# Pooled attention with a three-way maximum layer: tile 5's output by half products, and tile 6's first layer beside batch 7's scores alone

## The chip, the cores and the metric

The kernel runs on one core of a Trainium2 chip. The metric is device time in microseconds (us) of one execution, as the median of several runs. Its engines work in parallel, each through its own queue in order, and wait for one another through semaphores: TensorE (PE in the profile, its weight loads PEld) multiplies matrices into PSUM banks, VectorE (DVE) and ScalarE (ACT) read those banks and write SBUF, GpSimd (POOL) works on SBUF alone, and SyncE (SP) and POOL issue DMAs.

## The reference

```python
# q, k, v: 8 batches x 8 heads x 576 tokens x 64
k_p = k.reshape(B, H, 72, 8, D).mean(axis=3)          # groups of eight keys pooled
v_p = v.reshape(B, H, 72, 8, D).mean(axis=3)
attn = softmax(q @ k_p.T / 8)
x = (attn @ v_p), heads side by side                  # 4608 tokens x 512
h = max(max(x @ w1, x @ w2), x @ w3)                  # 768 wide
out = h @ w_out                                       # 4608 x 512, float32
```

## The kernel before

**Two grids.** Attention goes by batch (0 to 7, 576 tokens each), the two layers behind it by tile (0 to 8, 512 tokens each). The layers of tile n run beside the attention of batch n + 1, so that TensorE always has something to do while ScalarE takes exponentials. For one batch there are a key turn (`k`: POOL's pooled keys are turned by TensorE, and VectorE and ScalarE copy them to `kz`), eight scores steps (`s0` to `s7`; in the last stage nine, `s70` to `s78`, of 512 columns) each with an exp on ScalarE, and five values steps (`v0` to `v4`): eight small matmuls into `pav`, then a reciprocal and a multiplication on VectorE give `xn`, and step `x` turns it into `xT` by a DMA transpose on SyncE's queue. POOL folds the keys and values (`k7+1`, `v6+2` and the like: so many of the three steps of a fold).

**The first layer.** x @ w1 is folded into the output: w2 and w3 have w1 subtracted, so that the maximum is taken against zero, and w1 @ w_out (`wm`) is added in the output layer. For tiles 0 to 5 the first layer goes by "hidden" steps (`h` in a stage's list, `hidden_part`): twelve for a tile, each four matmuls of 512 columns, into banks `pw`, with a relu on ScalarE or a maximum on VectorE.

**Seven products.** A product of two-by-two blocks can be had from seven block products and some sums (Winograd's form). Tiles 6, 7 and 8 have their first layer that way (`seven`, products 1 to 7 for each of three column groups a, b, c: in the order, `6b` is product 6 of group b). Each is four matmuls of 256 columns for each of two weights. Products 1, 6, 5 and 3 of a group add up in one bank (`pA`), which ScalarE copies out after each of them (L811, L815) before the next is added. Product 2 has a bank of its own, `pB`, which VectorE adds (L782). Products 7, 5 and 4 use `pC`: 7 fills it, after 5 and 7 VectorE adds it to 5's copy, then 4 is added to it and VectorE adds it to 6's copy. VectorE's maxima (L785) then write `hT`. The sums that the products read come from `fold_x`: on VectorE for tile 6 (`T`, `U`), on POOL for tiles 7 and 8 (`T`).

**The output layer.** Tile n's output is [x, h] @ [wm, w_out]. The old form, `project(n)`, goes by four chunks of 128 tokens, each four and six matmuls of 512 columns into a bank `po`, one ScalarE copy and two stores; a step of it is written `F` and is one of these two halves. The other form, `out_seven(n)`, has seven products of ten matmuls of 256 columns into banks `oA`, `oB`, `oC`, with ScalarE's copies of `oA` (L737) and VectorE's additions (L740); it needs eight sums of x and h on VectorE (`a1` to `a4`, `b1` to `b4`). Before, tiles 2, 3, 4, 7 and 8 have it, and tiles 0, 1, 5 and 6 have the old one.

**The order.** It is written out by hand. `MIDDLE[n]` lists the steps of tiles 1 to 4 and `middle(n)` runs them; in it a number is an output product, `2l` and `2h` the halves of product 2, `e2` and `e5` VectorE's late additions, `7:T` and `6:k` a step of another batch. Tile 5 has `block(5, LEAD, ...)`: its twelve hidden steps with batch 6's scores and first two values between them. Then the last stage ("the weave") runs `ORDER`: tile 6's products, batch 6's other values, batch 7's scores and values, tile 7's products and tile 8's, with old-style output steps `F` of tile 5 (eight) and of tile 6 (six, the rest at the end) between them.

**Banks.** PSUM has eight banks. In the weave `pA` has two, `pB` and the scores share two ("sc"), and `pC` and `po` have one each; values and tile 7's `oA` share the other two. The weave's banks lie over those of the stages before it (scores and values 4, `pw` with `oB` and `oC` 3, `oA` 1), so a first use there waits until the old tile has been read.

Of the kernel before, what the change touches and what calls it, by code (L numbers as in the profile page):

```python
# [14 lines left out]
def kernel(  # L15
# [15 lines left out]
    B, H, S, D = q.shape  # L31
# [30 lines left out]
    def psum(shape, dtype, name, tag, bufs):  # L62
        return pools[-1].tile(shape, dtype, name=name, tag=tag, bufs=bufs)
# [86 lines left out]
    def tokens(t0, t1, k0=0, k1=KCH):  # L150

        t0, t1 = t0 % RING, (t1 - 1) % RING + 1
        assert t0 < t1
        return xT[:, k0:k1, t0:t1]
# [248 lines left out]
    def new_two():  # L403
        return sb3.tile([128, 2, C], F32, name="osb", tag="osb", bufs=3)

    def project(n):
        hT = hTs[n]
        for mm in range(4):
            m = 4 * n + mm
            last = m == TOK // 128 - 9  # L410
            if mm % 2 == 0:
                two = new_two()
            osb = two[:, mm % 2]
            for c in ((slice(0, C // 2), slice(C // 2, C)) if last else (slice(0, C),)):
                tag = PW if len(pools) < 3 else PA if last else PO
                po = psum([128, c.stop - c.start], F32, name="po", tag=tag[0], bufs=tag[1])
                for kc in range(KCH):
                    nc.tensor.matmul(po, tokens(128 * m, 128 * m + 128)[:, kc], wm_sb[:, kc, c],  # L418
                                     start=(kc == 0), stop=False)
                yield  # L420
                for jc in (0, 3, 1, 4, 2, 5):
                    nc.tensor.matmul(po, hT[:, jc, bass.ts(mm, 128)], wo_sb[:, jc, c],  # L422
                                     start=False, stop=(jc == JCH - 1))
                if c.start:
                    nc.vector.tensor_copy(out=osb[:, c], in_=po)
                else:
                    nc.scalar.copy(out=osb[:, c], in_=po)  # L427
                for u in range(2):
                    b, g = divmod(2 * m + u, NG)
                    dst = out[S * b:S * b + S, :].rearrange("(r g) c -> r g c", g=NG)  # L430
                    (nc.scalar if last and u else nc.sync).dma_start(
                        out=dst[:, GS[g], c], in_=osb[64 * u:64 * u + 64, c])
            yield
# [89 lines left out]
    def block(n, plan, parts):  # L523

        for slot, _ in enumerate(part for stage in parts for part in stage(n)):
            for b, steps in plan.get(slot, ()):
                if b < B:
                    do(b, steps)
# [5 lines left out]
    PRODUCTS = FIRST | {3: ("S4", 3), 4: (3, "T4"), 5: ("S1", "T1"), 6: ("S2", "T2")}  # L534
    sw = {}

    LEAD = {0: [(6, "s0")], 1: [(6, "s1")], 2: [(6, "s2")], 3: [(6, "s3")],
            4: [(6, "s4")], 5: [(6, "s5")], 6: [(6, "s6")], 7: [(6, "s7")],
            8: [(6, "v0 x0")], 9: [(6, "v1 x1")]}

    def minus(out, a, b):
        gate[:] = [nc.vector.tensor_tensor(out=out, in0=a, in1=b, op=ALU.subtract)]

# [39 lines left out]
    LAST = TOK // NB - 1  # L583
# [254 lines left out]
    def pool_step(n, name):  # L838
# [19 lines left out]
            held.clear()  # L858

    ORDER = """  # L860
        1a k7 F F T 2a U 1b v62 s70 F s71 s72 6a F s73 v63 5a 7a s74 s75 v64 F s76
        4a s77 3a s78 6b 2b 7b 1c v70 2c 5b T F 6c v71 3b F 5c 4b F v72 7c 3c 1a
        F 1b 4c v73 2a 2b 6b 6a F v74 5a 7a F 3a F T 1c 4a 5b 2c 6c 7b 3b F 5c
        4b F 1a 7c 2a 3c 6a 4c H 1b 2b 5a 6b 7a 3a h o1 1c 4a o2 5b 6c 7b 2c o6
        4b 3b 5c o5 7c o7 4c 3c o3 o4
    """

    def weave():

        products, seen = {}, {}  # L870
        for name in ORDER.split():
            if name == "F":
                next(tiles)
            elif name == "H":
                fold_h(LAST - 1)
                outs = out_seven(LAST - 1)
            elif name == "h":
                fold_h(LAST - 1, True)
            elif name[0] == "o":
                outs(int(name[1]), 0, 1)  # L880
            elif name[0] in "ksvx":
                b = int(name[1])
                do(b, name[0] + name[2:])
                if name[0] == "v" and b > 2:
                    do(b, "x" + name[2:])
                if name[0] == "s" and name[2] == "4" and b + 1 < B:
                    do(b + 1, "T")
            else:
                n = seen[name] = seen.get(name, 5) + 1
                if n not in products:  # L890
                    products[n] = seven(n)
                products[n](*((0, name == "U") if name in "TU" else
                              (int(name[0]), "abc".index(name[1]))))
                if name == "U":
                    held[:] = gate
                    pool_step(n, "v7+2")
# [17 lines left out]
        4: """  # L914
            h k k7< q7< v7< h a1 a3 a2 a4 f ! v5+2 h h s0 h s1 h s2 h s3 h s4 b1 f ! k6+1 h s5
            h s6 h s7 h b2 b3 b4 f ! k6+2 v6+1
            1 v0 x0 2l v1 x1 7:T 6 7 v2 x2 5 v3 x3 e5 2h 6:k 3 v4 x4 e2 4 v6+2 k7+3 v7+1
        """}
    folds = iter([f for wi in range(1, 3) for f in [fold_w(wi)] * 4])

    def middle(n):

        pieces, outs, out_tiles = hidden(n), None, project(n)
        for name in MIDDLE[n].split():
            if name == "h":
                next(pieces)
            elif name == "F":
                next(out_tiles)
            elif name == "f":
                next(next(folds))  # L930
            elif name == "!":
                held[:] = gate
            elif name.isdigit():
                outs = outs or out_seven(n)
                outs(int(name), 0, 1)
            elif name in ("2l", "2h"):
                outs = outs or out_seven(n)
                outs(2, "lh".index(name[1]))
            elif name in ("e2", "e5"):
                outs(int(name[1]))  # L940
            elif name[0] in "ab":
                sums_of(n, name)
            elif name[2:3] in ("<", "+"):
                pool_step(n, name)
            else:
                b, _, step = name.rpartition(":")
                do(int(b or n + 1), step)
        assert next(pieces, None) is None

    tt_all.append(const.tile([128, 4, 5, HALF], F16, name="tt", tag="tt"))  # L950
    for n in range(1, 5):
        middle(n)
    block(5, LEAD, (hidden,))
    assert next(folds, None) is None
    pad2 = const.tile([128, 3, 2, HALF], F16, name="pad2", tag="k16")
    pad3 = ld.tile([128, 8, 2, HALF], F16, name="pad3", tag="vt")
# [3 lines left out]
    stage.close()  # L960
    pools.append(ctx.enter_context(tc.tile_pool(name="psq", bufs=1, space=PSUM,
                                                reuse_waits="tile")))
    tiles = (t for n in range(5, LAST - 1) for t in project(n))
    weave()
    outs = out_seven(LAST)
    fold_h(LAST)
# [35 lines left out]
```

## Time and profile before

| | |
|---|---|
| median of 3 runs | 224.29 us (224.13 to 224.95) |
| the profiled execution | 224.51 us, its span 222.8 us |
| granted TensorE clock, mean | 0.998 |
| busy share: PE, DVE, ACT, POOL | 96%, 67%, 55%, 63% |
| tile 4's hidden layer, its output | 119.95 to 132.54, 132.54 to 141.65 us |
| tile 5's hidden layer | 141.65 to 154.66 us |
| the weave | from 154.66 us |

The span is what the profiler saw from the first to the last instruction; the rest of an execution's time lies around it. Times in the rows are us from the span's start. A row of the timeline is start, length, engine, line, operation, output <- inputs, and in square brackets how long the engine had been idle and for whom. A row of the chain is start, length, engine, tile, line and count. In the rows "x4" counts instructions.

### The profile page before, as it was taken

How to read it: one execution, taken by the hardware profiler on the slowest of the kernel's cores; microseconds unless marked ns; L12 is line 12 of the kernel's file. 1: busy time of each engine (PE TensorE's matmuls, PEld its weight loads, DVE VectorE, ACT ScalarE, POOL GpSimd, SP SyncE). 2: the span in 40 equal slices, each digit the busy share in tenths (PEclk: the TensorE clock that was granted, in tenths of full speed). 3: DMA queues.
4: the chain of work that ended last, by engine and by line, in shares of the span. 5: the costliest groups of instructions: out<-in, count | busy, mean ns of one | idle time of the engine just before them, and what ended most of it. 6: DMA issues, size and time to landing. Idle time of an engine off the chain costs nothing.

```text
span 222.8 us, 4685 instructions
## 1 busy us (share of the span) xinstructions
PE 215.0 (96%) x1807; PEld 146.9 (66%) x1807; DVE 149.0 (67%) x292; ACT 122.3 (55%) x221; POOL 141.0 (63%) x115
## 2 busy tenths in 40 slices
PE   7898999999999999999999999999999999999993
PEld 2477744558755555875597569655687777788882
DVE  4658967037584385787488658827677887898840
ACT  2267534756875478337823863584786545564340
POOL 7975404999949767787858766999421904772020
PEclk9999999999999999999999999999999999999999
DMA  6999999999469999649999999865341623200265
GB/s 175 212 197 197 203 208 203 201 239 230 86 112 204 222 188 216 114 93 160 233 227 170 154 269 144 157 133 118 76 100 27 139 62 74 47 3 0 68 197 163
DMA packets 50726, 33.54 MB, mean 151 GB/s; under 512 B 27056, under 2 KB 46384, under 8 KB 50704
## 3 DMA queue, kind: packets, MB, share of 16 engines
q0 software_dynamic: 20320, 16.98, 48.6%
q1 hardware_dynamic: 29936, 15.87, 31.0%
q10 hardware_dynamic: 448, 0.39, 0.7%
q8 instruction: 14, 0.23, 0.4%
q14 instruction: 8, 0.07, 0.1%
HBM read 34.60 MB, written 9.44 MB: 198 GB/s over the span
## 4 chain that ended last, share of the span: by engine, by line
PE 90%; DVE 4%; DMA 3%; ACT 1%; issue 1%; SPq 0%
PE pw L368 27%; PE oA L727 10%; PE po L422 9%; PE pA L805 7%; PE po L418 6%; PE psc L220 6%; PE oC L727 5%; PE pav L270 4%; PE pC L805 4%; DMA ktTrue<-in_k_dram 3%; PE oB L727 2%; PE pm L355 2%; PE pB L805 2%; PE pxt L261 2%; PE pqt L194 1%; DVE xn L278 1%
## 5 line engine op out<-in xcount | busy, mean ns | idle before, releaser
L368 PE MATMUL pw<-xT,mw 128*128 128x512 f16 (+1 forms) x336 | 72.8, 348 | 0.4 <-ACT xT L264 0.2
L368 PEld LDWEIGHTS <-mw 128*128 128x128 f16 x336 | 31.6, 98 | 20.7 <-issue 0.9
L376 DVE TENSOR_TENSOR hT<-t,pw 128x512 f16<-128x512 f16 (+1 forms) x42 | 25.4, 609 | 23.0 <-ACT et L225 16.4
L225 ACT ACTIVATE et<-psc 72x576 f16<-72x576 f32 (+2 forms) x54 | 35.2, 660 | 6.6 <-PE psc L220 6.3
L164 POOL TENSOR_TENSOR half<-half 96x768 f32<-96x768 f32 (+2 forms) x14 | 27.4, 1956 | 13.7 <-DVE rcp L276 9.0
L163 POOL TENSOR_TENSOR half<-vt 72x2048 f32<-72x2048 f16 (+1 forms) x8 | 28.6, 3577 | 3.3 <-DMA vt<-in_v_dram 2.7
L374 ACT ACTIVATE t<-pw 128x512 f16<-128x512 f32 (+1 forms) x42 | 22.6, 537 | 14.8 <-PE pw L368 14.1
L278 DVE TENSOR_TENSOR xn<-pav,rcp 128x512 f16<-128x512 f32 x40 | 27.7, 692 | 1.4
L422 PE MATMUL po<-mwo,hT 128*128 128x512 f16 (+1 forms) x102 | 23.5, 366 | 0.0
L220 PE MATMUL psc<-qT,kz 128*128 128x320 bf16 (+2 forms) x120 | 22.4, 278 | 0.8 <-DVE qT L196 0.6
L220 PEld LDWEIGHTS <-kz 128*128 128x128 bf16 x143 | 13.1, 98 | 13.3 <-ACT qT L196 1.1
L163 POOL TENSOR_TENSOR half<-ktFalse 96x1536 f32<-96x1536 f16 x6 | 18.8, 3128 | 4.0 <-issue 2.9
L811 ACT CAST pad<-pA 128x512 f16<-128x512 f32 x27 | 15.5, 587 | 8.2 <-PE pA L805 8.1
L276 DVE RECIPROCAL rcp<-pav 128x8 f32<-128x8 f32 x40 | 8.2, 204 | 17.0 <-PE pav L270 16.7
L270 PEld LDWEIGHTS <-et 72*128 72x128 f16 x320 | 15.3, 98 | 3.5 <-issue 0.3
L571 POOL TENSOR_TENSOR pad<-xT 128x256 f16<-128x256 f16 x8 | 6.1, 757 | 17.2 <-PE pB L805 8.6
L270 PE MATMUL pav<-vp,et 72*128 72x65 f16 x320 | 16.6, 194 | 0.1
L418 PE MATMUL po<-wm,xT 128*128 128x512 f16 (+1 forms) x68 | 16.6, 366 | 0.0
L737 ACT COPY osb<-oA 128x512 f32<-128x512 f32 x12 | 7.0, 585 | 16.7 <-PE oA L727 16.7
L427 ACT COPY osb<-po 128x512 f32<-128x512 f32 (+1 forms) x16 | 9.2, 572 | 12.0 <-PE po L422 12.0
L785 DVE SCALAR_TENSOR_TENSOR hT<-pad 128x512 f16<-128x512 f16 x18 | 14.1, 798 | 2.3 <-ACT pad L815 1.9
L805 PEld LDWEIGHTS <-sw 128*128 128x128 f16 x144 | 13.7, 98 | 2.4
(122 smaller groups left out, 382.9 us busy)
## 6 DMA issues: line engine op xcount, KB each, us to landing
out_dram<-osb SPq DMA_DIRECT2D x38, 128.0 KB, 5.5
ktFalse<-in_k_dram POOLq DMA_DIRECT2D x7, 576.0 KB, 8.7
qb<-in_q_dram POOLq DMA_DIRECT2D x7, 576.0 KB, 12.7
vt<-in_v_dram POOLq DMA_DIRECT2D x6, 576.0 KB, 14.9
mw<-in_moe_w_dram POOLq DMA_DIRECT2D x9, 256.0 KB, 9.2
out_dram<-osb SPq DMA_DIRECT2D x8, 256.0 KB, 5.6
ktTrue<-in_k_dram SPq DMA_DIRECT2D x3, 384.0 KB, 5.0
vt<-in_v_dram POOLq DMA_DIRECT2D x4, 288.0 KB, 12.4
```

The lines of the kernel that those rows point to most:

```text
L163: yield e.tensor_tensor(out=f, in0=t[:, :, 0:4, :], in1=t[:, :, 4:8, :], op=ALU.add)
L164: yield e.tensor_tensor(out=f[:, :, 0:2, :], in0=f[:, :, 0:2, :], in1=f[:, :, 2:4, :], op=ALU.add)
L220: nc.tensor.matmul(out, kz_all[b % 2][f % 2][rows, h, :], qTs[b][rows, n + i0:n + i1, 64 * (h % 2):64 * (h % 2) + 64], start=True, stop=True)
L225: nc.scalar.activation(out=out, in_=in_, func=FT.Exp, scale=1.0 / 64.0)
L270: nc.tensor.matmul(pav[:, h // 4, 65 * (h % 4):65 * (h % 4) + 65], ets[b][:, h, c0:c0 + 128], vp_all[:, b, h, :], start=True, stop=True)
L278: nc.vector.tensor_tensor(out=xn, in0=pv[:, :, :, 0:D], in1=rcp.to_broadcast([128, 2, 4, D]), op=ALU.mult)
L368: mm = nc.tensor.matmul(pw, w_sb[wi][:, kc, bass.ts(jc, 128)], x[:, kc], start=(kc == 0), stop=(kc == KCH - 1))
L376: nc.vector.tensor_tensor(out=hT[:, jc, c0:c1], in0=t, in1=pw, op=ALU.max)
L418: nc.tensor.matmul(po, tokens(128 * m, 128 * m + 128)[:, kc], wm_sb[:, kc, c], start=(kc == 0), stop=False)
L422: nc.tensor.matmul(po, hT[:, jc, bass.ts(mm, 128)], wo_sb[:, jc, c], start=False, stop=(jc == JCH - 1))
L727: nc.tensor.matmul(p, left, right, stop=(r == 4), skip_group_check=True, start=(i in FIRST and r == 0 and (m == 0 or n == LAST)))
L805: mm = nc.tensor.matmul(p[:, w], a[:, kc, bass.ts(g, 128)], b[:, kc, :], start=(i in FIRST and w + kc == 0), stop=(w + kc == 2), skip_grou ...
```

## The change

Tile 5 loses its `LEAD` block and gets a list in `MIDDLE`, like tile 4's: hidden steps with batch 6's scores, the eight sums, then the seven output products with all five values of batch 6 and the key turn of batch 7 between them. The folds of values 6, keys 7 and values 7, which stood at the end of tile 4's list, stand in tile 5's. In the weave's `ORDER` the key turn, three values steps of batch 6 and the eight `F` steps of tile 5 are gone. Up to tile 6's product 4c no `F` is left: tile 6's products stand with batch 7's scores, later its first four values, and tile 7's first products. Tile 6's six `F` steps stand further on, with the gaps between them changed.

```diff
-    LEAD = {0: [(6, "s0")], 1: [(6, "s1")], 2: [(6, "s2")], 3: [(6, "s3")],
-            4: [(6, "s4")], 5: [(6, "s5")], 6: [(6, "s6")], 7: [(6, "s7")],
-            8: [(6, "v0 x0")], 9: [(6, "v1 x1")]}
-
...
     ORDER = """
-        1a k7 F F T 2a U 1b v62 s70 F s71 s72 6a F s73 v63 5a 7a s74 s75 v64 F s76
-        4a s77 3a s78 6b 2b 7b 1c v70 2c 5b T F 6c v71 3b F 5c 4b F v72 7c 3c 1a
-        F 1b 4c v73 2a 2b 6b 6a F v74 5a 7a F 3a F T 1c 4a 5b 2c 6c 7b 3b F 5c
-        4b F 1a 7c 2a 3c 6a 4c H 1b 2b 5a 6b 7a 3a h o1 1c 4a o2 5b 6c 7b 2c o6
+        1a T 2a U 1b s70 s71 6a s72 s73 5a 7a s74 s75 s76
+        4a s77 3a s78 6b 2b 7b 1c v70 2c 5b T 6c v71 3b 5c
+        4b v72 7c 3c 1a 1b 4c v73 2a 2b 6b F 6a v74 5a 7a F 3a F T 1c 4a 5b 2c 6c 7b 3b F 5c
+        4b F 1a 7c 2a 3c 6a F 4c H 1b 2b 5a 6b 7a 3a h o1 1c 4a o2 5b 6c 7b 2c o6
         4b 3b 5c o5 7c o7 4c 3c o3 o4
     """
...
         4: """
             h k k7< q7< v7< h a1 a3 a2 a4 f ! v5+2 h h s0 h s1 h s2 h s3 h s4 b1 f ! k6+1 h s5
             h s6 h s7 h b2 b3 b4 f ! k6+2 v6+1
-            1 v0 x0 2l v1 x1 7:T 6 7 v2 x2 5 v3 x3 e5 2h 6:k 3 v4 x4 e2 4 v6+2 k7+3 v7+1
+            1 v0 x0 2l v1 x1 7:T 6 7 v2 x2 5 v3 x3 e5 2h 6:k 3 v4 x4 e2 4
+        """,
+        5: """
+            h h a1 a3 a2 a4 ! v6+2 h h s0 h s1 h s2 h s3 h s4 b1 ! k7+1 h s5
+            h s6 h s7 h b2 b3 b4 ! k7+2 v7+1
+            1 v0 x0 2l v1 x1 6 7 v2 x2 5 v3 x3 e5 v4 x4 2h 7:k 3 e2 4
         """}
...
-    for n in range(1, 5):
+    for n in range(1, 6):
         middle(n)
-    block(5, LEAD, (hidden,))
...
-    tiles = (t for n in range(5, LAST - 1) for t in project(n))
+    tiles = project(LAST - 2)
     weave()
```

## The prediction

> **What bounds the kernel now.** I read the busy time by stretches first, for tile 4's hidden layer and output stage and the start of the weave, then the chain.
>
> ```profile
> 119.95:132.54 12.59, 12.59 (x71) 6.51 (x69) 8.00 (x16) 9.19 (x16) 9.20 (x7) 1.00 1.05 182
> 132.54:141.65 9.11, 9.09 (x114) 8.06 (x112) 8.16 (x18) 2.13 (x5) 6.53 (x4) 1.00 0.84 141
> ...
> 154.66:164.90 10.24, 10.24 (x96) 6.92 (x94) 6.99 (x15) 7.37 (x14) 5.48 (x3) 1.00 0.37 78
> 164.90:175.30 10.40, 10.40 (x100) 7.88 (x98) 8.33 (x15) 6.62 (x12) 3.51 (x5) 1.00 0.33 70
> ```
>
> The columns are length, then busy us of PE, PEld, DVE, ACT, POOL, then clock. TensorE fills every stretch, the weave from 154.66 too, where tile 6's products stand between the halves of tile 5's old-style output (po). So TensorE time saved is time saved, and a TensorE wait made is time lost. VectorE (6.99 of 10.24, 8.33 of 10.40) and ScalarE (7.37 at first) have room there only because po gives TensorE other work. The chain gives the unit prices:
>
> ```profile
> 132.54 1.09 PE oA L727 x10
> ...
> 157.82 0.44 PE pA L805 x4
> 158.26 0.26 PE pav L270 x8
> 158.52 0.22 PE psf L220 x2
> 158.74 0.86 PE po L418 x4
> ...
> 189.71 1.30 PE po L422 x6
> ```
>
> **TensorE's work.** Removed: tile 5's four po chunks, 4 x (0.86 + 1.30) = 8.64 us. Added: seven products of ten matmuls, 7 x 1.09 = 7.63. The three value steps (0.26 each) and the scores only move; the key turn is made earlier. Net -1.01 us.
>
> **Work that hides.** Tile 5's stage becomes a copy of tile 4's: hidden steps with scores, then products with values. It adds to VectorE eight sums and three additions, to ScalarE nothing (four copies for four). In tile 4's stretches the same work left VectorE at 8.00 of 12.59 and 8.16 of 9.11 with TensorE full, so I cost it at nothing; uncovered, it would cost up to that 8.16 us. POOL's folds of batches 6 and 7 move from ahead of that stage into it, as batches 5 and 6 lie in tile 4's: 9.20 of 12.59, nothing; their last two steps must land before batch 7's first values, 10 us into the weave, and the stretch from 154.66 shows them with slack. SyncE gets five transposes earlier and six stores for eight: nothing.
>
> **The entry of the weave.** Tile 4's output stage passes into a hidden layer with other banks. Tile 5's now passes into product 1a, whose bank (pA) is the one that tile 5's outputs (oA) leave: the built program makes 1a wait for ScalarE's last oA copy. Before, tile 4's end:
>
> ```profile
> 138.08 0.43 PE L270 MATMUL pav<-vp,et 72*128 72x65 f16 x8
> 138.79 0.69 DVE L278 TENSOR_TENSOR xn<-pav,rcp 128x512 f16<-128x512 f32 x1
> 139.40 0.68 DVE L740 TENSOR_TENSOR osb<-osb,oC 128x512 f32<-128x512 f32 x1
> 139.99 0.97 DVE L210 COPY kz<-pkt 64x288 bf16<-64x288 bf16 x2
> 140.99 0.21 DVE L276 RECIPROCAL rcp<-pav 128x8 f32<-128x8 f32 x1
> 141.24 0.69 DVE L278 TENSOR_TENSOR xn<-pav,rcp 128x512 f16<-128x512 f32 x1
> ...
> 141.33 0.97 ACT L210 COPY kz<-pkt 64x288 bf16<-64x288 bf16 x2 [2.46 <-DVE rcp L276]
> 142.32 0.58 ACT L737 COPY osb<-oA 128x512 f32<-128x512 f32 x1
> ```
>
> ScalarE's kz copies wait for VectorE's, and the oA copy is behind them: it ends at 142.90, 1.25 us after TensorE went on to tile 5's hidden layer at 141.65, where I set the end of that stretch. Nobody waited for it. Now 1a does: 1.3 us as the row stands. In the new order VectorE normalises the fifth values (0.21 + 0.69) before kz, at most 0.9 later, so 2.2 at most. Counted through, VectorE ends kz as product 4 ends; ScalarE follows at about 0.1 with 0.99, then 0.58, so 1a starts at 1.70. I take 1.7. Besides, the key turn now stands after the fifth values and takes the bank of the fourth's, so it waits for their xn: by the rows that ends 1.40 after the fourth values start (138.08 to 139.48), and TensorE comes there after 2 x 0.26 and half a product, 0.55, 1.07: 0 to 0.4 late, I take 0.4. **Entry: +2.1.**
>
> **Tile 6's products without po between.** What each step waits for is in the code and the built program. Products 1, 6, 5, 3 of a group sum up in one pA bank, each after ScalarE's copy of the one before. A group's 4 waits for VectorE's addition of 5+7, the next group's 7 for its addition of 4 (one bank). Two "sc" banks serve the scores and product 2, so a score waits for the exp (or addition) two users back. The latencies and rates:
>
> ```profile
> 21.32 0.58 ACT L264 COPY xT<-pxt 128x512 f16<-128x512 f16 x1 [0.22 <-PE pxt L261]
> 21.95 1.47 PE L368 MATMUL pw<-xT,mw 128*128 128x256 f16 x12 [0.19 <-ACT xT L264]
> ...
> 154.50 0.60 PE L805 MATMUL pA<-xT,mw 128*128 128x256 f16 x4
> 155.13 0.58 ACT L811 CAST pad<-pA 128x512 f16<-128x512 f32 x1 [0.70 <-PE pA L805]
> 157.22 0.60 PE L805 MATMUL pB<-xT,mw 128*128 128x256 f16 x4
> 157.93 0.69 DVE L782 TENSOR_TENSOR pad<-pad,pB 128x512 f16<-128x512 f16 x1 [0.67 <-PE pB L805]
> 158.34 0.58 ACT L811 CAST pad<-pA 128x512 f16<-128x512 f32 x1 [0.33 <-PE pA L805]
> 158.54 0.42 DVE L571 TENSOR_TENSOR pad<-xT 128x512 f16<-128x512 f16 x1
> 158.82 0.59 ACT L225 ACTIVATE et<-psf 72x512 f16<-72x512 f32 x1
> ```
>
> ScalarE starts 0.63 after a product starts (154.50 to 155.13), works 0.58, and TensorE goes on 0.05 after its end (21.90 to 21.95): 1.26 us from one product on a pA bank to the next, of which TensorE works 0.44. Queued behind each other, ScalarE starts an operation each 0.48 (158.34 to 158.82), VectorE each 0.61 (157.93 to 158.54).
>
> I count from the end of tile 5's product 4. 1a starts at 1.70, 2a at 2.14, 1b at 2.58, score 0 at 3.02. Score 1 needs 2a's bank: 1a's copy ends at 2.92, the addition at 3.66, so it starts at 3.71, **0.47 late**. 6a 3.93, score 2 4.37; score 3 needs score 1's exp, which stands behind 1b's copy and score 0's exp on ScalarE, until 4.84 (**0.25**); 5a needs 6a's copy, behind those, 5.32 (**0.26**). 7a, scores 4 and 5 are ready; score 6 needs score 4's exp, behind 5a's copy and two exps: 7.29 (**0.65**). 4a, 7, 3a, 8, 6b, 2b, 7b, 1c follow at 0.44 or 0.22 each, and the first values of batch 7 start at 10.6. Their predecessors are 12 x 0.44 + 9 x 0.22 = 7.26 us of work, so 3.35 are lost, 1.70 of them the entry. **+1.6.**
>
> From there VectorE sets the pace: each group wants three additions, two maxima and a normalisation. 3b waits 0.13, 5c 0.05, values 2 0.22 (bank of values 1), 7c **0.96** (the maximum of 3b, the normalisation and the addition of 4b are queued ahead), tile 7's 1b 0.39 (3c's copy), 6b 0.22 (POOL's sums of tile 7, below), 5a 0.57 (6a's copy, no po ahead of it). **+2.5.** Then po of tile 6 stands between products as before, and I add nothing. The sums of tile 7 go by
>
> ```profile
> 168.51 0.69 DVE L278 TENSOR_TENSOR xn<-pav,rcp 128x512 f16<-128x512 f32 x1
> 171.71 0.67 POOL L571 TENSOR_TENSOR pad<-xT 128x256 f16<-128x256 f16 x1 [8.59 <-ACT pad L811]
> 175.86 0.67 POOL L571 TENSOR_TENSOR pad<-xT,pad 128x256 f16<-128x256 f16 x1
> ```
>
> 2.5 us from batch 7's first xn (ends 169.20) through its transpose to the first sum, 4.8 to the end of the sixth (176.53), which 6b needs. The walk has that xn end at 12.0 after product 4, so the sixth sum ends at 19.3, 0.2 after TensorE comes to 6b.
>
> **Sum.** -1.0 + 2.1 + 1.6 + 2.5 = +5.2. The profiled execution took 224.51 (span 222.8 and 1.7 around it) against a median of 224.29: the span becomes 228.0, that execution 229.7, the median **229.5**.
>
> **Bounds of the unshown waits.** No stretch of before runs these products without po, so the engines' loads bound their cost from below. For a maximum there are two prices, beside POOL's sums and alone:
>
> ```profile
> 174.04 1.22 DVE L785 SCALAR_TENSOR_TENSOR hT<-pad 128x512 f16<-128x512 f16 x1
> 174.04 0.67 POOL L571 TENSOR_TENSOR pad<-xT,pad 128x256 f16<-128x256 f16 x1
> 178.64 0.69 DVE L785 SCALAR_TENSOR_TENSOR hT<-pad 128x512 f16<-128x512 f16 x1
> ```
>
> If VectorE never waited: two leftover additions 1.3, four sums at 0.42 1.7, nine additions at 0.68 6.1, six maxima at 0.69 4.1, three normalisations at 0.90 2.7 = 15.9 us, against TensorE's 13.1 to tile 7's 1b (23 products, 9 scores, 4 values); with the 0.61 spacing about 14.6. ScalarE: the leftover 1.65, 14 copies at 0.58, 9 exps at 0.59 = 15.1. So the least loss is 1.5 to 2.8, net of the 1.01 saved +0.5 to +1.8. The walk stands above since each wait starves the next engine. Upward goes the first price of a maximum (rival b).
>
> **Rivals.**
> (a) *Pure load*: queues run full ahead of TensorE and only the busier engine's total counts: the middle of the bounds, +1.2, 225.5. For it: additions and maxima of different groups are independent. Against: one pC bank and two sc banks forbid running ahead. Chance 0.12.
> (b) *POOL's sums of tile 7 collide with VectorE's maxima*, now on the path: by the rows above; four of them fall into those sums, 4 x 0.53 = 2.1: +7.3, 231.6. Against: between those rows stand maxima beside POOL that did not stretch. Chance 0.10. The Trainium skill, "SBUF — State Buffer", Who interferes with whom, states that a VectorE instruction with two SBUF inputs and a GpSimd instruction that reads SBUF hold one port in turn, whoever is second being blocked whole; the rows at 174.04 agree in direction, and by the rule all four would collide.
> (c) *Not slower*: the waits are all hidden because ScalarE and VectorE come early out of tile 5's stage (their tails end before product 4 does), and the two pA banks cover the rest; only -1.0 is left: 223.3. It decides if the last oA copy ends less than about 0.1 after product 4; the row at 142.32 speaks against. Chance 0.04.
> (d) *The clock falls* because TensorE idles in short pieces. In before a stretch with holes kept it:
>
> ```profile
> 0.00:6.00 6.00, 4.47 (x11) 1.44 (x12) 2.25 (x5) 1.28 (x1) 4.71 (x13) 1.00 0.70 184
> ```
>
> At half clock the stretch's 13.1 us of work would take 26.2, of which the 6.2 of waits cover some: +6.9 on the forecast, 236.4. Chance 0.02. The Trainium skill, "TensorE: Matmul & The Clock Gate", HAM oscillation, states that an idle window of about 3.4 us halves the clock, and that frequent short idling between bank cycles did it in one kernel; the row above shows clock 1.00 at 4.47 busy of 6.00 and does not agree.
>
> **Numbers.** The forecast's case (+3.5 to +7) holds 0.72: 227.8 to 231.3, for the entry's 1.3 to 2.2, the key turn's 0 to 0.4 and a third more or less on the two walks. (a) and (c) lie below it, (b) and (d) above. From 226.5 to 232.0 lie the forecast, the top of (a) and most of (b), 0.82. Slower by over 0.5% (what a measurement here can tell, 1.1 us): the forecast, (b), (d) and the upper 0.07 of (a), 0.91; within: the rest of (a) and half of (c), 0.07; faster: 0.02.
>
> **What would show it.** Right: TensorE idle at tile 6's 1a for 1.3 to 2.2 us behind ScalarE's oA copy; TensorE waits on psf, pA, pC lines, 0.2 to 1 us each, summing to some 6 us between tile 5's outputs and tile 7's 5a; tile 5's stage full; from there on full. Wrong: the 1a wait absent, or that span full, or waits in tile 5's hidden layer, or a clock under 1.00.

## The result, and the profile after

The changed kernel took **230.74 us** (median of 4 runs, 230.41 to 230.97), the kernel before 224.22 (224.13 to 224.95): **ratio 1.0273, 95% interval 1.0255 to 1.0290**. The forecast was 229.5 with a range of 226.5 to 232.0. The profiled execution took 230.87 with a span of 229.2, against 224.51 and 222.8; TensorE's clock was 0.997. Line numbers are four lower than before (`LEAD` is gone): L801 is a first-layer product, L807 and L811 ScalarE's copies, L778 VectorE's additions, L781 its maxima, L733 and L736 copy and addition of an output product, L567 the sums.

The busy time by stretches (columns: length, PE, PEld, DVE, ACT, POOL, clock, DMA share, GB/s), cut where the walk cut it: tile 5's hidden layer; its output; from its product 4 to batch 7's first values; on to the last wait; the rest.

```profile
141.93:154.46 12.53, 12.53 (x66) 6.33 (x67) 6.68 (x13) 9.34 (x17) 7.47 (x4) 1.00 0.62 144
154.46:163.84 9.38, 9.07 (x113) 8.04 (x112) 7.96 (x18) 1.86 (x5) 6.81 (x4) 1.00 0.28 58
163.84:174.28 10.44, 8.06 (x73) 6.52 (x71) 6.37 (x12) 9.15 (x18) 3.71 (x3) 1.00 0.44 108
174.28:189.04 14.76, 12.66 (x124) 9.39 (x122) 12.84 (x23) 6.85 (x13) 6.36 (x8) 1.00 0.21 42
189.04:215.42 26.38, 26.38 (x223) 21.71 (x222) 20.98 (x31) 13.93 (x25) 12.55 (x16) 1.00 0.14 31
```

Tile 5's stage is full but for one wait (0.31 us here, 0.47 by what follows), the two stretches behind it are not, and from 189.04 TensorE is full again. A caution on the column: a product of four matmuls with the next right behind it takes 0.44 us (the chain), but its row shows 0.60, since the last matmul's end is modelled. A group ahead of a wait so counts 0.16 too much as busy, and each wait below is really 0.16 longer than it is shown. What TensorE waited for in the changed kernel (total, times, longest):

```profile
PE pA L801 <- ACT osb L733: 1.4, 1, 1.4
...
PE pC L801 <- DVE pad L778: 0.8, 1, 0.8
...
PE psf L220 <- ACT et L225: 0.5, 1, 0.5
PE pA L801 <- ACT pad L807: 0.4, 1, 0.4
PE pA L801 <- POOL pad L567: 0.3, 1, 0.3
PE pkt L201 <- DVE xn L278: 0.3, 1, 0.3
PE psf L220 <- DVE pad L778: 0.3, 1, 0.3
PE pA L801 <- ACT pad L811: 0.2, 1, 0.2
PE po L418 <- ACT osb L427: 0.2, 1, 0.2
```

None of these nine stood in the kernel before. Seven of them are 0.2 to 0.5 us, and with 0.16 added to each all nine are 6 us. Another 1.1 us lies in six gaps too short for this list, which only the starts of neighbouring steps show: at score 3 and at tile 6's 5a, 3b, 5c and 4c, and at values 2 of batch 7 (`v72`). The first wait is the entry of the weave; the timeline shows how it comes about:

```profile
161.53 0.29 PE L201 MATMUL pkt<-ident,kp 96*128 96x96 bf16 x3 [0.31 <-DVE xn L278]
...
162.74 0.96 DVE L210 COPY kz<-pkt 64x288 bf16<-64x288 bf16 x2
...
163.79 0.96 ACT L210 COPY kz<-pkt 64x288 bf16<-64x288 bf16 x2 [3.01 <-DVE kz L210]
...
164.78 0.59 ACT L733 COPY osb<-oA 128x512 f32<-128x512 f32 x1
...
165.41 0.60 PE L801 MATMUL pA<-xT,mw 128*128 128x256 f16 x4 [1.41 <-ACT osb L733]
...
174.28 0.42 PE L270 MATMUL pav<-vp,et 72*128 72x65 f16 x8
...
189.04 1.02 PE L418 MATMUL po<-wm,xT 128*128 128x512 f16 x4 [0.24 <-ACT osb L427]
```

VectorE's `kz`, ScalarE's `kz`, ScalarE's copy of `oA`, product 1a: each starts where the one before ends. VectorE's `kz` doesn't start right behind the key turn, which ended at 161.82; it stands behind the normalisation of the fifth values (162.13, 0.69 us) on VectorE's queue. TensorE, which ended product 4 at 163.84 (without the modelled end), stands until 165.41. The last two rows are the marks by which the runs below are compared: batch 7's first values, and the po step that still waits.

By these marks the difference is made up so (work at 0.44 a product, 0.22 a score, 0.26 a values step, 0.86 and 1.30 the halves of a po chunk):

| term | forecast | measured |
|---|---|---|
| TensorE's work | -1.01 | -1.01 (taken over, not measured apart) |
| tile 5's hidden layer starts (141.65 before, 141.93 after) | 0 | +0.28 |
| key turn (0.31 in the trace, and the 0.16) | +0.4 | +0.47 |
| 1a behind product 4 | +1.7 | +1.57 |
| 1a to first values: 8.87, work 7.26 | +1.6 | +1.61 |
| first values to the po step: 14.76, work 11.38 | +2.5 | +2.98, and 0.40 at the po step |
| sum | +5.2 | +6.3 |

The spans differ by 6.4. About 0.1 of that I can't place.

### The profile page after: what moved, and what is told of

Same layout as the page of the kernel before. It is cut to its first block, busy times and chain, and to the rows that moved or that the text cites. A ratio compares the mean times of both kernels' runs of the same rounds, so it can differ in the third digit from the quotient of the medians.

```text
span 229.2 us, 4754 instructions
## 1 busy us (share of the span) xinstructions
PE 215.9 (94%) x1836; PEld 149.6 (65%) x1837; DVE 153.0 (67%) x303; ACT 122.3 (53%) x221; POOL 141.4 (62%) x115
## 4 chain that ended last, share of the span: by engine, by line
PE 79%; issue 5%; DVE 4%; ACT 4%; DMA 4%; POOL 3%; POOLq 0%; ACTq 0%; DVEq 0%
PE pw L368 26%; PE oA L723 11%; PE po L422 7%; PE oC L723 5%; PE psc L220 5%; PE pA L801 5%; PE po L418 4%; DMA vt<-in_v_dram 4%; PE pav L270 4%; PE oB L723 3%; PE pC L801 2%; PE pm L355 2%; POOL pad L567 2%; PE pxt L261 2%; ACT et L225 2%
## 5 line engine op out<-in xcount | busy, mean ns | idle before, releaser
L807 ACT CAST pad<-pA 128x512 f16<-128x512 f32 x27 | 15.6, 588 | 10.4 <-PE pA L801 8.2
L733 ACT COPY osb<-oA 128x512 f32<-128x512 f32 x16 | 9.4, 586 | 21.2 <-PE oA L723 21.2
L422 PE MATMUL po<-mwo,hT 128*128 128x512 f16 (+1 forms) x78 | 17.7, 363 | 0.0
L801 PEld LDWEIGHTS <-sw 128*128 128x128 f16 x144 | 13.9, 98 | 4.5 <-issue 2.2
L778 DVE TENSOR_TENSOR pad<-pad,pC 128x512 f16<-128x512 f16 x18 | 12.3, 683 | 6.8 <-PE pC L801 4.0
L723 PEld LDWEIGHTS <-tt 128*128 128x128 f16 x160 | 15.0, 98 | 1.7
L781 DVE SCALAR_TENSOR_TENSOR hT<-pad 128x512 f16<-128x512 f16 x18 | 13.9, 788 | 2.7 <-ACT pad L811 2.4
L567 POOL TENSOR_TENSOR pad<-xT 128x256 f16<-128x256 f16 x8 | 6.7, 834 | 11.0 <-ACT pad L807 6.8
```

What stands on the lines that cost most here:

```text
L723: nc.tensor.matmul(p, left, right, stop=(r == 4), skip_group_check=True, start=(i in FIRST and r == 0 and (m == 0 or n == LAST)))
L801: mm = nc.tensor.matmul(p[:, w], a[:, kc, bass.ts(g, 128)], b[:, kc, :], start=(i in FIRST and w + kc == 0), stop=(w + kc == 2), skip_grou ...
```

## Experiments

The kernel before was run beside each group: 224.3 to 224.6 us. "After" is the changed kernel, 230.74.

**1. Is it the seven products, or the bare tile 6 behind them?** Tile 5's output goes back to the old form, in its own stage, and POOL's folds go back to the end of tile 4's list; the weave stays as in after.

```diff
-    for n in range(1, 6): middle(n)
+    for n in range(1, 5): middle(n)
+    block(5, LEAD, (hidden, project))     # LEAD with 13: v2, 14: v3, 15: v4 of batch 6, 17: k of batch 7
```

> The weave's order is that of the changed kernel, but tile 5's output keeps the old form (four po chunks), run in tile 5's own stage with values 2 to 4 and the key turn between them: the second half of the change alone. TensorE's work is as before, 1.0 us more than in the changed kernel. Theory (the loss is tile 6's products left without other TensorE work, plus the entry behind tile 5's oA copies): the entry wait of 1.6 us and the key turn's 0.3 go, the waits among tile 6's products and scores (1.6 as forecast) fall a little because VectorE comes in without two leftover additions, those after them (2.5) stay: 224.2 + 3.5 to 4.5 = 227.7 to 228.7 us. Rival 1 (the loss lies in the seven products of tile 5 and their sums): about 224.2. Rival 2 (all of it is the bare stretch, and the entry wait only hides waits that come anyway): 230.7 + 1.0 = 231.7.

Measured **229.48 us** (229.18 to 229.91), ratio 1.0226 (1.0205 to 1.0248), a miss by 0.8. In the timeline 1a came in without a wait, but tile 6 waited as before:

```profile
164.45 0.60 PE L806 MATMUL pA<-xT,mw 128*128 128x256 f16 x4
...
166.50 0.38 PE L220 MATMUL psf<-qT,kz 128*128 128x64 bf16 x3 [0.35 <-DVE pad L783]
...
170.04 0.38 PE L220 MATMUL psf<-qT,kz 128*128 128x128 bf16 x3 [0.47 <-ACT et L225]
173.32 0.42 PE L270 MATMUL pav<-vp,et 72*128 72x65 f16 x8
```

From 1a to the first values it took 173.32 - 164.45 = 8.87 us, exactly as in after. The forecast had hoped that without the entry ScalarE would be ahead by then. It wasn't: its last po copy (164.66) still stood ahead of 1a's copy (165.14). So without any seven products for tile 5 the cost is 229.48 - 224.52 = 5.0 us: taking work out from between tile 6's products is what costs, whatever form it goes to. The key turn and three values steps leave the weave too in this run; the next one puts po alone back.

**2. Put the cover back.** After, with tile 5's eight po steps in the weave a second time, without their stores.

```diff
-        1a T 2a U 1b s70 s71 6a s72 s73 5a 7a s74 s75 s76
-        4a s77 3a s78 6b 2b 7b 1c v70 2c 5b T 6c v71 3b 5c
-        4b v72 7c 3c 1a 1b 4c v73 2a 2b 6b F 6a v74 ...
+        1a F F T 2a U 1b s70 F s71 s72 6a F s73 5a 7a s74 s75 F s76
+        4a s77 3a s78 6b 2b 7b 1c v70 2c 5b T F 6c v71 3b F 5c 4b F v72 7c 3c 1a
+        F 1b 4c v73 2a 2b 6b 6a F v74 ...
```

> The changed kernel, and besides, the eight old-form half steps of tile 5 stand again where they stood before in the weave; they compute tile 5's output a second time, and their stores are left out. TensorE gets 8.6 us of work more. Theory: they cover the waits among tile 6's products again, so the time is that of before and the seven products' 7.6 us, plus the entry wait (1.6) and the key turn's (0.3), which lie ahead of the first such step: 224.2 + 9.5 = 233.7, 3.0 over the changed kernel. Rival (TensorE's waits are not among those steps, or the extra copies of po on ScalarE make as many): 230.7 + 8.6 = 239.3.

Measured **234.47 us** (234.19 to 234.93), ratio 1.0449 (1.0429 to 1.0469): 0.8 above the theory, 4.8 below the rival. Of the waits only the entry (1.4) and the key turn (0.3) are left; the stretch behind the first values is full:

```profile
178.05:192.00 13.95, 13.95 (x133) 10.11 (x131) 11.14 (x22) 7.27 (x13) 6.49 (x8) 1.00 0.17 34
```

8.64 us of TensorE work cost 3.7: the other 4.9 fell into waits. That is the sum of the lines 1.61 + 2.98 + 0.40 above, within 0.1.

**3. The entry alone.** Product 3 goes ahead of the key turn.

```diff
-            ... v4 x4 2h 7:k 3 e2 4
+            ... v4 x4 2h 3 7:k e2 4
```

> The changed kernel with output product 3 of tile 5 ahead of the key turn instead of behind it, so that ScalarE's last oA copy is queued ahead of its kz copies. Theory: product 1a no longer waits (1.6 us less there), but its copy on ScalarE is then behind the kz copies and the addition of 2a behind VectorE's leftovers, so that the next wait, at score 1, takes part of it back: 1.0 us faster than the changed kernel, 229.7. Rival 1 (the entry wait is lost time in full): 229.1. Rival 2 (everything behind it is paced by VectorE, so nothing is won): 230.7.

Measured **229.71 us** (229.55 to 229.96), ratio 1.0233 (1.0214 to 1.0252), as expected. ScalarE copies `oA` before `kz`, so 1a and the key turn wait no more, and the next in line does, on VectorE's last addition of tile 5:

```profile
PE pB L801 <- DVE osb L736: 1.1, 1, 1.1
```

Of 2.0 us of entry 1.0 is won by an exchange of two names; the rest moves to another queue.

**4. to 6. Can the seven products be the cover?** Three tries to spread tile 5's output products through the weave in place of po, which keeps the 1.0 us of saved work. The first puts VectorE's eight sums (`a1` to `b4`) into tile 5's hidden layer, where before had none:

```diff
+            h s0 h s1 h s2 a1 a3 a2 a4 h s3 h s4 h s5 h s6 b1 h s7 h v0 x0 h v1 x1 h h b2 b3 b4
...
-        1a T 2a U 1b s70 s71 6a s72 s73 5a 7a s74 s75 s76
+        1a k7 p1 T 2a U 1b v62 s70 pl ph s71 s72 6a pe s73 v63 5a 7a s74 p6 s75 v64 s76
...
```

> Tile 5's output by seven products as in the changed kernel, but its ten steps stand in the weave where the old-form steps stood before, three products before batch 7's first values and four after, with their banks taken from po and the scores' two; batch 6's values 2 to 4 and the key turn stay in the weave as before, the eight sums go to tile 5's hidden layer. Theory (seven products save 1.0 us of TensorE, and what costs is only the missing cover): 224.2 - 1.0 = 223.2, up to 0.8 more where VectorE's three added additions (0.6 each) come late. Rival (VectorE's and the banks' load of the second form costs more than TensorE saves, wherever it stands): 225 to 227.

Measured **233.69 us** (233.38 to 234.65), ratio 1.0420 (1.0392 to 1.0447). The timeline of that hidden layer:

```profile
147.06 3.15 POOL L163 TENSOR_TENSOR half<-ktFalse 96x1536 f32<-96x1536 f16 x1
147.18 5.25 DVE L616 TENSOR_TENSOR tt<-xT,tt 128x512 f16<-128x512 f16 x2
...
153.08 1.86 PE L368 MATMUL pw<-xT,mw 128*128 128x512 f16 x4 [4.15 <-DVE hT L376]
```

Two sums that need 0.88 us in the other kernels took 5.25 beside POOL's folds, everything behind them on VectorE came late, TensorE stood 4.15 us, and afterwards four matmuls took 1.86 in place of 1.03: the clock had halved. So this run says nothing on the cover. Theory and rival both missed what `!` does in the lists of tiles 2 to 4 and in the change: it holds POOL's next fold until VectorE's sums are done.

The second has that gate, and the sums of the hidden half in the weave:

```diff
+            h s0 h s1 a1 a3 a2 a4 ! v6+2 k7+3 h s2 h s3 h s4 h s5 h s6 h s7 h v0 x0 h v1 x1 h h
...
+        1a p1 T 2a U k7 1b v62 pl ph B 6a pe v63 s70 s71 5a 7a ...   # B: b1 b3 b2 b4, then v7+3 gated
```

> Tile 5's seven output products are spread through the weave in place of po, as in e4_products_spread, but the sums no longer meet POOL's folds: the sums of the token half stand after the second hidden step with a gate before POOL's next fold, the sums of the hidden half stand in the weave after batch 7's key turn with a gate before batch 7's value fold. Theory (what costs time in the change is tile 6's products standing bare, and e4 was lost to the port alone): TensorE's work is 1.0 us under that of the kernel before and its cover is as good, so 223.3 to 224.5 us, no wait of 4 us on hT in tile 5's hidden layer and clock 1.00. Rival (VectorE has no room in the weave for eight sums and three additions more, so the spread products wait as the bare ones do): 226 to 229 us, with TensorE waiting on VectorE's pad and osb lines.

Measured **235.75 us** (235.25 to 236.41), ratio 1.0510 (1.0484 to 1.0536), another miss. The hidden layer was full, but the fold of batch 7's values, now behind `B`, came too late for ScalarE, whose copy of 1b goes into the tile that this fold reads:

```profile
163.19 4.05 POOL L163 TENSOR_TENSOR half<-vt 72x2048 f32<-72x2048 f16 x1 [6.91 <-issue]
...
167.27 1.07 ACT L808 CAST pad<-pA 128x512 f16<-128x512 f32 x2 [6.12 <-POOL half L163]
```

The third gives that copy a tile of its own and orders sums and folds one behind the other:

```diff
+        1a B p1 2a k7 T 1b pl ph U pe p6 6a s70 s71 v62 5a 7a ...    # v7+3 gated behind U
...
-            return (pad3[:, 4] if odd else pad2[:, 0]) if i == 1 else ...
+            return (pad5 if odd else pad2[:, 0]) if i == 1 else ...
```

> Tile 5's seven output products spread through the weave a third time, now with POOL's folds of batch 7's keys ended before VectorE's sums of the hidden half start, its fold of batch 7's values behind tile 6's sums, and a tile of its own (1 KB a partition) for 1b's copy, which in e5_spread_gated waited for that fold. Theory (bare products cost, the port and the buffer lost e4 and e5): TensorE's work is 1.0 us under before's; VectorE has eight sums and three additions more to do at the head of the weave (about 9 us of work for TensorE's 10), so some waits stay: 223.3 to 225.0 us, no wait above 1 us, clock 1.00. Rival (VectorE has no room): 226 to 229 us with VectorE busy over 9 of 10 us through the first 20 us of the weave.

Measured **233.02 us** (231.57 to 233.83), ratio 1.0356 (1.0314 to 1.0397). Now POOL's fold lies beside tile 6's maxima:

```profile
165.83 2.35 POOL L164 TENSOR_TENSOR half<-half 72x1024 f32<-72x1024 f32 x1
...
166.34 4.07 DVE L782 SCALAR_TENSOR_TENSOR hT<-pad 128x512 f16<-128x512 f16 x2
...
171.90 0.38 PE L220 MATMUL psf<-qT,kz 128*128 128x256 bf16 x2 [2.66 <-DVE pad L779]
```

Two maxima took 4.07 us for 1.29 elsewhere. Neither theory nor rival of these three runs held: a full VectorE isn't it either (in the third, 8.30, 6.16 and 8.32 of 10 us from 155 to 185). What follows is narrower: in before, POOL's folds of batch 7's keys and the longest step of its values (152.47 to 156.53) lie beside tile 5's hidden layer and the first two us of the weave, where VectorE has no sums to do but one at the very end. Seven products for tile 5 bring eight sums, and in the three orders tried these folds either met the sums (the first) or moved into tile 6's time (the other two). Whether a version of this kind without any such overlap would beat before stays open.

**7. and 8. Where must cover stand?** After with four po steps (4.3 us) back, either ahead of 6a, or behind batch 7's first values.

```diff
-        1a T 2a U 1b s70 s71 6a s72 s73 5a ...
+        1a F F T 2a U 1b s70 F s71 6a F s72 s73 5a ...          # first half
```
```diff
-        ... 1c v70 2c 5b T 6c v71 3b 5c 4b v72 7c 3c 1a 1b ...
+        ... 1c v70 2c 5b T F 6c v71 3b F 5c 4b F v72 7c 3c 1a F 1b ...   # second half
```

> The changed kernel, with two of tile 5's four po chunks back as filler (4.3 us of TensorE work, not stored), all ahead of tile 6's 6a and score 2, in the first half of the bare stretch. Theory (each wait is local: about 1.6 us of waits up to batch 7's first values and about 3.3 us behind them, and filler covers only those near it): 230.74 + 4.32 - 1.6 = 233.5 us (233.0 to 234.0), the waits on psf and 5a of the first half gone and those behind the first values (7c, 1b, 6b, 5a, the po step) unchanged. Rival (one backlog of VectorE and ScalarE that runs through both halves, so that time given early is also won later): 230.7 to 231.5 us, with the later waits gone too.

> The changed kernel, with two of tile 5's four po chunks back as filler (4.3 us, not stored), behind batch 7's first values, among 6c, 5c, v2 and 1b. Theory (local waits): 230.74 + 4.32 - 3.3 = 231.8 us (231.3 to 232.4), the waits of the first half unchanged and those of 7c, 1b, 6b and 5a gone. Rival (the second half's waits come from work left over by the first, so filler that comes after it covers no more than the first half's share): 233.3 to 234 us.

Measured **234.13 us** (234.00 to 234.31) and **234.10 us** (233.62 to 234.22), ratios 1.0437 (1.0418 to 1.0455) and 1.0431 (1.0410 to 1.0451). The first lies 0.6 above the theory's middle and 0.1 above its range, the second 2.3 above the middle, where its rival would put it; so the rows must say what happened. Filler in the first half:

```profile
165.07 0.60 PE L801 MATMUL pA<-xT,mw 128*128 128x256 f16 x4 [1.41 <-ACT osb L733]
...
174.35 0.38 PE L220 MATMUL psf<-qT,kz 128*128 128x128 bf16 x3 [0.59 <-ACT et L225]
...
177.63 0.43 PE L270 MATMUL pav<-vp,et 72*128 72x65 f16 x8
...
192.17 1.02 PE L418 MATMUL po<-wm,xT 128*128 128x512 f16 x4 [0.24 <-ACT osb L427]
```

From 1a to the first values 12.56 us for 8.87 + 4.32 = 13.19: 0.63 covered, about what score 1 (0.46) and 5a had waited. Score 6's wait, behind the filler, is still there (0.59 for 0.48), and nearly the whole second half too (14.54 us to the po step for 14.76). There is no backlog that an early lead would work off: the rival is out. Filler in the second half:

```profile
173.87 0.42 PE L270 MATMUL pav<-vp,et 72*128 72x65 f16 x8
...
190.50 1.02 PE L418 MATMUL po<-wm,xT 128*128 128x512 f16 x4 [0.24 <-ACT osb L427]
```

16.63 us for 14.76 + 4.32: 2.45 covered, of the 3.3 forecast; 5a (0.41) and the po step (0.24), which stand behind the filler, wait as before. From 1a to this mark the run takes 1.87 longer than after, not 3.36, so the rival is out here too. Most of the rest comes at the very end (from the last matmul's start to the end of the span 5.85 us for 4.61), with the last po copy of ScalarE:

```profile
224.03 3.52 ACTq L666 DMA_DIRECT2D out_dram<-ob  x2
...
227.59 0.37 ACT L427 COPY osb<-po 128x256 f32<-128x256 f32 x1 [3.59 <-PE po L422]
```

The issue of two stores took 3.52 us on ScalarE's queue (1.40 in after), and the last copy stood behind it. Why it did so only here stays open. Both runs say the same: a wait is covered by TensorE work that stands right ahead of it, and by none further off. One thing they don't separate: the filler gives ScalarE two po copies more in the same stretch (0.59 us each), so a part of what stayed uncovered may be theirs.

**9. Rival (b), the collision of POOL's sums for tile 7 with VectorE's maxima.** After without these sums; tile 7 reads tile 5's.

```diff
+        if n == LAST - 1:
+            return {f"T{i + 1}": tt_all[0][:, i, 0:2] for i in range(4)}
```

> The changed kernel without POOL's eight sums for tile 7: its products take tile 5's sums in their place, so tile 7's output isn't the reference's. Theory (the walk): only 6b's wait for those sums goes, 0.3 to 0.5 us, and the maxima that stretched beside them were hidden: 230.2 to 230.5 us. Rival b of the prediction (the maxima beside POOL's sums are on the path): the two maxima of 0.92 and 0.97 and the one of 1.19 fall back to 0.69, 1.0 us, with the wait of 7c for them: 229.2 to 229.7 us.

Measured **230.21 us** (229.95 to 230.43), ratio 1.0258 (1.0237 to 1.0279): 0.5 won, the size that the theory gave. The timelines of after and of this run:

```profile
179.00 0.92 DVE L781 SCALAR_TENSOR_TENSOR hT<-pad 128x512 f16<-128x512 f16 x1
179.01 0.60 PE L801 MATMUL pC<-pad,sw 128*128 128x256 f16 x4 [0.76 <-DVE pad L778]
...
180.68 0.68 DVE L778 TENSOR_TENSOR pad<-pad,pC 128x512 f16<-128x512 f16 x1
...
181.41 0.60 PE L801 MATMUL pC<-pad,mw 128*128 128x256 f16 x4
...
183.57 0.49 PE L801 MATMUL pA<-pad,sw 128*128 128x256 f16 x3 [0.33 <-POOL pad L567]
```
```profile
179.25 0.69 DVE L785 SCALAR_TENSOR_TENSOR hT<-pad 128x512 f16<-128x512 f16 x1
179.27 0.60 PE L805 MATMUL pC<-pad,sw 128*128 128x256 f16 x4 [0.76 <-DVE pad L782]
...
180.70 0.68 DVE L782 TENSOR_TENSOR pad<-pad,pC 128x512 f16<-128x512 f16 x1
...
181.44 0.60 PE L805 MATMUL pC<-pad,mw 128*128 128x256 f16 x4
```

Without POOL's sums the three maxima take 0.69 (0.92, 0.97 and 1.19 in after), so the collision is real. 7c (the second row of each) waits 0.76 in both, so this run's rival, by which that wait goes, is out. But two other waits go, and not only the one that the theory named. One is 6b's for POOL's sums (0.33 in the last row of after, 0.49 in all). The other is that of tile 6's 4c, too short for the list of waits: 4c starts 0.69 us after tile 7's 1b in after (180.72 to 181.41) and 0.46 here (180.98 to 181.44), and a product takes 0.44. 4c needs VectorE's addition of 7c (180.68, 180.70), which starts 1.68 us behind the maximum in after and 1.45 here. From the first values to the po step the run takes 14.04 us for 14.76: 0.23 less at 4c, 0.49 at 6b. In experiment 3, too, the maximum at this place took 0.69, 4c didn't wait, and the stretch was 14.52 us. So VectorE's side of the collision is on the path, for some 0.2 us of the 2.1 that rival (b) priced. POOL's side counts too: its second and fifth sums took 1.00 and 1.11 us for 0.67 beside these maxima, and 6b waited for the sixth, which ended at 183.52. With 0.63 us from one sum to the next, as where none stretched, it would have ended at about 182.6, before TensorE comes to 6b; that is an estimate from these rows.

The Trainium skill, "SBUF — State Buffer", Who interferes with whom, has VectorE instructions with two SBUF inputs and POOL instructions that read SBUF exclude each other: this run and the first and third spread ones agree.

**10. Banks?** Po's idle bank is lent to 2a (so that the scores keep both "sc" banks) and to 7b and 4b (so that `pC` alternates).

```diff
+                if n == 6 and (of, g) in (("B", 0), ("C", 1)):
+                    tag = PO
```

> The changed kernel with po's bank, which stands idle until tile 6's first po step, lent to tile 6's product 2a (in place of an sc bank) and to products 7b and 4b (in place of the only pC bank). Score 1's wait for the addition of 2a (0.30 in the record, 0.46 with the matmul's modelled end) goes by any theory. The 7c wait (0.76, or 0.92) tells them apart. Theory of the walk (VectorE sets the pace of the second half; in the changed kernel it was busy 7.92 of 8.20 us from 174.6 to 182.8): the wait only moves on to 4c or 1b, so 230.1 to 230.5 us. Rival (the single bank is the limit, VectorE could have run later): both go, 230.74 - 0.46 - 0.92 = 229.4 us (229.2 to 229.6).

Measured **230.66 us** (230.46 to 230.76), ratio 1.0271 (1.0249 to 1.0293): nothing, a little less than even the theory gave. The waits of score 1 and 7c are gone, and the timeline shows two new ones:

```profile
168.04 0.86 PE L220 MATMUL psf<-qT,kz 128*128 128x128 bf16 x5 [0.33 <-ACT et L225]
...
181.13 0.60 PE L803 MATMUL pC<-pad,mw 128*128 128x256 f16 x4 [0.78 <-DVE pad L778]
```

Score 2 waits for an exp, 4c for an addition. From 1a to the first values it is 8.87 us once more (165.36 to 174.23). The banks only name the wait; the queues behind them set it.

**11. ScalarE's load?** The copies of 1a, 6a and 5a of tile 6 go to VectorE.

```diff
-                nc.scalar.copy(out=kept(i, g), in_=p)
+                (nc.vector.tensor_copy if n == 6 and g == 0 else nc.scalar.copy)(out=kept(i, g), in_=p)
```

> The changed kernel with three of tile 6's copies, those of 1a, 6a and 5a, on VectorE in place of ScalarE. In the changed kernel ScalarE was busy 9.15 of the 10.44 us from tile 5's last product to batch 7's first values, VectorE 6.37. Theory (in the first half ScalarE's queue sets the pace, whatever the banks, as e10_po_bank_lent showed for the banks): of the 1.6 us lost there behind the entry, about 1 us goes, the waits of score 6 (0.48) and 5a first, and part of it is lost again to VectorE behind the first values: 229.9 to 230.4 us. Rival (the waits are the latency of each product's copy and exp, on whichever engine, so no load moved helps): 230.6 to 231.2 us.

Measured **231.12 us** (230.96 to 231.23), ratio 1.0292 (1.0278 to 1.0306): no faster than after (1.0255 to 1.0290), where the rival put it; the theory fell. ScalarE was busy 7.46 us for 9.15 in the same stretch, and TensorE waited longer:

```profile
167.90 0.38 PE L220 MATMUL psf<-qT,kz 128*128 128x64 bf16 x3 [0.99 <-ACT et L225]
```

Score 6's wait hadn't changed (0.46), and that of score 1, in the row, had grown: 1a's copy, now on VectorE, stands there ahead of tile 6's first sums and 2a's addition, which ran from 167.25 to 167.93 (in after the sums were done before 1a's copy came). The trace names an exp that ended at 167.84 as the releaser; the addition ended at about the same time, and which of the two decided is open. What is left as the cause is the length of the chain from product through copy or exp to the next user of its bank, in queues that run in order; that is argued from what the other runs exclude, not tried by itself.

**12. All mends together**, 3, 10 and 11.

> All that the runs before suggest for mending the change where it stands: product 3 ahead of batch 7's key turn (e3_product3_before_key: 1.0 us won), po's idle bank lent (e10_po_bank_lent: 0.1), the three copies on VectorE (e11_copies_on_vector: 0.3 to 0.8 if its theory holds). Theory (bare products cost what the engines' pace sets, and only the entry can be won back): 228.7 to 229.4 us, still about 2% slower than the kernel before. Rival (the entry and the bare stretch lose to the same queue of ScalarE, so the two mends together win more than their sum): 227.0 to 228.3 us.

Measured **229.82 us** (229.78 to 229.93), ratio 1.0235 (1.0221 to 1.0249). No more than the third run alone won: 0.4 above the theory, 1.5 above the rival.

## Why the prediction was right

- **What bounds the kernel** (TensorE full, VectorE and ScalarE with room only because po gives TensorE other work): right, and the core of it. Experiment 2 gave the cover back, and the waits behind the entry were gone; experiments 1, 7 and 8 placed it.
- **TensorE's work, -1.01**: no run contradicts it. Experiment 1, which has po's work and no entry wait, is 1.26 below after, against 1.57 + 0.47 - 1.01 = 1.03 by these terms, and 0.21 of the rest lies behind the first values (14.55 us for 14.76).
- **Work that hides, 0**: right. Tile 5's hidden layer is full (12.53 of 12.53) and its output stage too, but for the key turn. The gates that keep POOL off VectorE's sums were part of that cover, which the prediction did not say; experiment 4 shows what they are worth.
- **The entry, 1.7 and 0.4**: 1.57 and 0.47. The chain from VectorE's `kz` to 1a is the one that was counted. The key turn's wait lies just above its bound of 0.4.
- **First half, +1.6**: 1.61, and each step came within 0.2 us of the count: score 1 at 3.57 (3.71), 5a at 5.21 (5.32), score 6 at 7.16 (7.29), the first values at 10.44 (10.6) behind product 4.
- **Second half, +2.5**: 2.98. 7c waited 0.92 with its 0.16 (0.96 forecast), tile 7's 1b 0.40 (0.39), 5a 0.57 (0.57); 3b, 5c and values 2 together 0.41 by their starts (0.40). The excess is in two steps: 6b 0.49 (0.22), since POOL's sums ended a little later than the walk had them, and tile 6's 4c 0.25, which the walk had at nothing. Experiment 9 shows that 4c's wait comes from the collision of rival (b).
- **"I add nothing" behind 5a**: wrong. Only product 3a stands between the second half of tile 6's first po chunk and the first half of the next, which has to wait until ScalarE has copied the single po bank: 0.24 in the row, 0.40 in all. Before, the same two places in the order held the two halves of one chunk.
- **The sum, +5.2**: 1.2 short, of which 0.5 are the second half, 0.4 the po step, 0.3 the start of tile 5's stage, which lies ahead of the change, less 0.1 at the entry; some 0.1 stay unplaced. The misses mostly add up, so the time isn't met by errors that cancel.
- **Rivals.** (a), pure load: out; it gave 225.5. VectorE was busy 12.84 of 14.76 us and ScalarE 9.15 of 10.44 where TensorE waited, and moving load (experiment 11) or lending banks (10) won nothing. (Its bound counts 23 products and four values, which reach to tile 6's 4c and batch 7's fourth values, not to tile 7's 1b as it says.) (b): real, and on the path for some 0.2 us on VectorE's side, not 2.1 (experiment 9). (c): out, the `oA` copy ended 1.53 us after product 4 (164.78 + 0.59 to 163.84). (d): out for this change, the clock was 1.00 through all its waits, the longest 1.57; in the spread runs with waits of 2.66 and more it came true. The row of the first 6 us that the prediction set against (d) doesn't bear that reading: its one hole is the 1.53 us ahead of the first matmul, and the ten matmuls of 512 columns behind it take 4.38 us, 0.44 each, where later ones take 0.22 (four hidden matmuls in 0.86). TensorE ran there at half its later pace, though the clock column shows 1.00.

## What to carry to other kernels

Work that looks removable on the bounding engine may be the cover for the latencies of the others: before taking 1 us out of it, walk the steps that then stand next to each other, product by product, with the measured latency of each copy and exp. Cover was local here: it had to stand right ahead of the step that would wait, and neither a bank more nor an engine less loaded replaced it. And a sum moved on VectorE is to be placed against POOL's work as carefully as against its own queue; a wait of 0.2 us that comes of such a meeting stands in no list of waits, only in the starts of the steps.

## What the runs showed of the hardware

**A wait of 2.66 us halved TensorE's clock for some 3.4 us.** In the third spread run, the stretches of that wait and behind it:

```profile
170.00:171.90 1.90, 0.00 (x1) 0.00 (x0) 1.81 (x4) 0.00 (x0) 0.00 (x0) 1.00 0.00 0
171.90:173.00 1.10, 1.10 (x9) 0.92 (x9) 0.00 (x0) 0.69 (x2) 0.00 (x0) 0.87 0.49 99
173.00:174.00 1.00, 1.00 (x7) 0.72 (x5) 0.00 (x0) 0.39 (x1) 0.00 (x0) 0.50 0.18 39
...
176.00:177.00 1.00, 1.00 (x16) 0.90 (x15) 0.78 (x2) 0.19 (x1) 0.00 (x0) 0.93 0.00 0
```

The means of 0.87 and 0.93 put the fall at 172.7, 0.8 us after TensorE has begun again, and the return at 176.1. In the first spread run it fell within the idle stretch of 4.15 us. The Trainium skill, "TensorE: Matmul & The Clock Gate", What's actually happening, gives one idle window of about 3.4 us for the fall and one busy window of that length for the return. The return agrees; for the fall a stretch of 2.66 us sufficed here, though TensorE had also been idle for 0.37 and 0.69 us in the 4 us ahead of it. The same page's section on depth-cycling through PSUM queues tells of a kernel in which frequent short idling between matmul groups made the clock swing. After, with nine waits of 0.4 to 1.6 us in 28 us, doesn't show it: its clock stayed at 1.00.

**Beside POOL's folds, VectorE's operations on two SBUF inputs stretched until the folds ended**: a sum of 0.55 us took 4.16 (first spread run), two maxima 4.07 for 1.29 (third), while in the same stretches VectorE's operations with an input in a PSUM bank kept their 0.69.
